# Attention and a two-layer feed-forward product: the second product of three token blocks as seven block products

## The chip, the cores and the metric

The kernel runs on one core of one Trainium2 chip. The metric is the time of one execution on the device in microseconds (us). Engines are called as the profile calls them: PE (matrix engine, PEld its weight loads), DVE (vector), ACT (scalar), POOL (GpSimd), SP (the queue that issues nearly all DMAs).

## The reference

Chunked attention gives x (3072 tokens by 512), and x goes through two matrix products with a piecewise activation in between. All is float32.

```python
out[:, :, c_start:c_end] = softmax(scale * q_c @ k_full^T) @ v_full   # 32 queries, 64 keys with 8 memory keys, head size 64
...
h = x @ w_in                                   # (3072, 512) @ (512, 2048)
g = np.where(h >= 1, h, np.where(h <= -1, 0.0, (h + 1) ** 2 / 4.0))
return g @ w_out                               # (3072, 2048) @ (2048, 512)
```

## The kernel before

**Tiles.** Tokens go in six blocks of 512. The 2048 middle columns are 16 chunks of 128, and four of them make a "quad" (q 0 to 3; m = 2q and 2q+1 are pairs of an even and an odd chunk). Each float32 operand is held as a high part and a rest, both in the matrix engine's reduced format, and each product is three: high by high, high by rest, rest by high. `weights` (L175) finds a chunk's weights, all of which lie in SBUF for the whole run in 16 tiles `wr` (printed as `wr_<number>`).

**Blocks 0 and 1** are worked with eight block products for everything, in the order of the table `FIRST` (L27). That stage also decodes the weights (`decode`, L184) and, in `build` (L563, letter t in the table), forms four combinations of each pair of w_in chunks and writes them to HBM as `saved`.

**Blocks 2 to 5** run the table `QUADS` (L61), one string per quad, through `quad` (L765). The first product (x by w_in) uses the seven-product scheme: `product` (L665) multiplies one sum of x's quarters (`A11`, `A12`, `A22`, `S1` to `S4`, made by `sum_up` and `split`, L642 and L647) with one w_in piece or combination. Such a product is 12 matmuls of 256 columns, seven to a quad. Three of the seven pieces are resident; the other four (products 6, 5, 7, 4) are loaded from `saved` by `load_t` (L591) into places of w_in that are no longer needed ("holes", L550), each load in two DMAs of 256 KB whose rows end as 1 KB pieces.

All seven go to two PSUM banks, X and Y (`PROD`, L51): `copy_out` (L711, ACT) copies X after products 1, 6 and 7, `add_up` (L719, DVE) adds Y, `relus` (L724) is three ACT operations, `join` (L735) one on DVE. The product that adds to a bank next waits for those that read it.

The second product (g by w_out) splits each g tile (128 by 512) into high part (`high`, L740, ACT) and rest (`low`, L746, DVE), and `pe_out` (L684) multiplies with eight products: 12 matmuls of 512 columns for one g tile, 16 tiles to a block. In the table it stands between the products of X and Y, and covers their waits; most of it belongs to the same quad or the one before. Results gather in four PSUM banks, and `store` and `last_store` (L519, L526) copy them out. The attention of the next block (`attention`, L405; its two PE parts are `pe_scores` and `pe_values`) is strewn between.

**What sets the order.** `InOrder` (L81) keeps every engine in the order in which the code emits, so the tables set the order on each engine; SP's DMAs too go one after the other, and one that waits holds those behind it. Since all operations go through it, the profile gives L89 for nearly all.

Of the kernel before, what the change touches and what calls it, by code (L numbers as in the profile page):

```python
# [16 lines left out]
P = 128  # L17
# [7 lines left out]
SECOND = 2  # L25

# [19 lines left out]
    F11 F12 n3 n3 F13 F13 F11 + n3 F12 n3 F13 n3 n3 n2 F14 F14 F14 n3 F13 F15 F12 n3 + F14 F13 F14  # L46
    n3 n2 F13 F15 F15 F15 F15 n3
# [13 lines left out]
QUADS = (  # L61
    """
    @S0 -h12 p1 p2 -g22 0 -l12 c1 p6 a11 0 -g12 p5 r11 0 z0 dS4 c2 m11 p7 kS4 c3 h11 a22 0 -g21 r22
    z1 m22 l11 h22 p4 r21 0 p3 a12 l22 0 0 r12 m21 h21 l21 g11 m12
    """,
    """
    p1 -h12 p2 0 0 c1 a11 0 -g21 p6 c2 -l12 0 r11 m11 0 -g22 p7 p5 0 @V0 c3 -g12 a22 h11 r22 p4 p3
    0 m22 h22 l11 a12 r12 g11 @S1 l22 r21 m21 h21 l21 m12
    """,
    """  # L70
    1 p2 p1 c1 1 a11 -g22 r11 m11 1 1 1 p6 p5 -h12 c2 -g21 p7 -l12 -g12 c3 h11 a22 1 r22 l11 m22 1
    h22 p4 l22 r21 p3 m21 h21 1 a12 r12 m12 1 g11 1 l21 1
    """,
    """
    p1 p2 c1 1 p6 -g22 -g21 c2 a11 1 kA11 @V1 r11 kA12 1 -h12 p7 m11 -l12 h11 c3 p5 dS3 a22 p4 p3
    dS1 r22 dS2 l11 m22 h22 -g12 g11 l22 a12 kA22 r21 m21 r12 m12 h21 kS3 kS2 l21 kS1
    """,
)
# [16 lines left out]
def attn_ffn_kernel(ctx: ExitStack, tc: tile.TileContext, first_qk, first_v, qk, vw, w, out):  # L95
# [34 lines left out]
    def two_banks(tag, name):  # L130
        return ps_2.tile([P, 2, 512], F32, name=name, tag=tag)
# [52 lines left out]
    def decode(i):  # L184
# [15 lines left out]
        hi, lo = ws[i][:, 0:n2], ws[i][:, n2 : 2 * n2]  # L200
# [204 lines left out]
    def attention(key):  # L405

        pe_scores(key)
        yield
# [5 lines left out]
        pe_values(key)  # L414
        yield
# [19 lines left out]

    items = []

    def half_step(blk, half, fc):
# [8 lines left out]
        for i, (m, x, cc) in enumerate(terms):  # L447
            pe.matmul(hp, m[:, cc * P : (cc + 1) * P], x[:, cc], start=i == 0, stop=i == len(terms) - 1)
# [24 lines left out]
        for t in range(2):  # L473
            ts, to = slice(t * P, (t + 1) * P), acc[blk][2 * half + t]
            for i, (a, m) in enumerate(((gh, wh), (gh, wl), (gl, wh))):
                pe.matmul(to, a[:, ts], m, start=fc == 0 and i == 0, stop=False)
        yield

    def step(blk, fc):
# [5 lines left out]
        for i, (m, x, cc) in enumerate(terms):  # L485
            pe.matmul(hp, m[:, cc * P : (cc + 1) * P], x[:, cc], start=i == 0, stop=i == len(terms) - 1)
# [39 lines left out]
    def last_store(t):  # L526

        src = acc[NB - 1][t]
        r0 = (NB - 1) * TB + t * P
        if t == 1:  # L530
            for i, (copy, queue) in enumerate(((dve.tensor_copy, sp), (act.copy, act))):
                cols = slice(i * DM // 2, (i + 1) * DM // 2)
                ob = apool.tile([P, DM // 2], F32, name="ob", tag=("pr", "f")[i], bufs=1 + i)
                copy(ob, src[:, cols])
                queue.dma_start(out[r0 : r0 + P, cols], ob)
        else:
            ob = apool.tile([P, DM], F32, name="ob", tag={2: "qk", 3: "v", 0: "pt"}[t])
            (act.copy if t == 3 else dve.tensor_copy)(ob, src)
            sp.dma_start(out[r0 : r0 + P, :], ob)

# [9 lines left out]
    hole_of = {}  # L550
    for i, n in ((0, 0), (1, 2), (2, 4), (3, 6)):
        for s in range(2):
            hole_of[i, s] = 2 * (n + s) + 1

    def hole(i, s):
        j, k = place[0, hole_of[i, s]]
        w = ws[j].rearrange("p (a b c) -> p a b c", a=2, b=2)
        return w[:, :, k, 0:HQ]

    saved = dram.tile([NFC // 2, P, 4, 2, HQ], F32, name="saved")  # L560
    ahead = {}

    def build(m):  # L563
# [5 lines left out]
        fef = apool.tile([P, 2, 2, HQ], F32, name="fef", tag="f", bufs=2)  # L569
        for j in range(2):  # L570
            hi, lo = (weights(0, 2 * m + j, part).bitcast(F32) for part in range(2))
            dve.tensor_tensor(fef[:, j].rearrange("p a b -> p (a b)"), hi, lo, op=ALU.add)
            yield
        b11, b21, b12, b22 = (fef[:, j, k] for j in range(2) for k in range(2))
        tf = apool.tile([P, 4, HQ], F32, name="tf", tag="f", bufs=2)
        dve.tensor_tensor(tf[:, 1], b12, b11, op=ALU.subtract)
        yield
        dve.tensor_tensor(tf[:, 2], b22, b12, op=ALU.subtract)
        yield
        dve.tensor_tensor(tf[:, 0], b22, tf[:, 1], op=ALU.subtract)  # L580
        yield
        dve.tensor_tensor(tf[:, 3], b21, tf[:, 0], op=ALU.subtract)
        yield
        st = ahead["y0"].tile([P, 4, 2, HQ], F32R, name="st", tag="st")
        act.copy(st[:, :, 0], tf)
        yield
        dve.tensor_tensor(st[:, :, 1], tf, st[:, :, 0].bitcast(F32), op=ALU.subtract)
        sp.dma_start(saved[m], st.bitcast(F32))
        yield

    def load_t(i, q):  # L591
        for s in range(2):
            sp.dma_start(hole(i, s).bitcast(F32), saved[2 * q + s, :, i])
# [3 lines left out]
    def side(name):  # L597
        if name not in part_of:
            if name in ("A11", "A12"):
                both = ahead["y0"].tile([P, 2, 2, 2, HQ], F32R, name="sa", tag="st")  # L600
                part_of["A11"], part_of["A12"] = both[:, 0], both[:, 1]
            else:
                pool = ahead["y0" if name == "S2" else "y1"]
                part_of[name] = pool.tile([P, 2, 2, HQ], F32R, name=name.lower())
        return part_of[name]

    def x_plain(key):

# [46 lines left out]
    def stationary(i, q, s, part):  # L655
        m = 2 * q + s
        if i == 1:
            return weights(0, 2 * m, part)[:, 0:HQ]
        if i == 2:
            return weights(0, 2 * m, part)[:, HQ : 2 * HQ]  # L660
        if i == 3:
            return weights(0, 2 * m + 1, part)[:, HQ : 2 * HQ]
        return hole(PROD[i][2], s)[:, part]

    def product(i, q):  # L665
        to, name, _ = PROD[i]
        x = side(name)
        for s in range(2):
            terms = [(0, 0, cc) if lo == 0 else (0, 1, cc) for cc in range(2) for lo in range(2)]
            terms += [(1, 0, cc) for cc in range(2)]  # L670
            for n, (wp, xp, cc) in enumerate(terms):
                pe.matmul(
                    bank[to][:, s * HQ : (s + 1) * HQ],
                    stationary(i, q, s, wp)[:, cc * P : (cc + 1) * P],
# [4 lines left out]
                )  # L679

# [286 lines left out]
```

## Time and profile before

| | us |
|---|---|
| median of 3 runs | 600.39 (599.39 to 600.58) |
| the profiled execution | 599.33 |
| its span, first to last instruction | 597.6 |

Busy over the span: PE 579.3, PEld 501.4, DVE 395.5, ACT 333.0, POOL 0.7 us. Block 2's first product starts at about 224 us; blocks 2, 3 and 4 then repeat every 93 us.

A row of the grouped instructions reads: line, engine, operation, output<-inputs, shapes, count | busy time, mean ns of one | idle time of the engine before it. A matmul's own duration holds the time of its results' way out; what a stream of matmuls costs is read from the chain of work, whose rows are start, length, engine and count. A row of the stretches gives, for each engine, busy us and the number of instructions, then the granted clock of PE, the busy share of the 16 DMA engines, and GB/s.

### The profile page before, as it was taken

The numbers are of one execution on the slowest core, as the hardware profiler recorded it, in microseconds if no ns is written. First come the engines' busy times: TensorE is split into PE (matmuls) and PEld (weight loads), VectorE is DVE, ScalarE is ACT, GpSimd is POOL, SyncE is SP. The second block draws the span as 40 slices with busy tenths as digits, with TensorE's granted clock in tenths as the row PEclk, the third lists the DMA queues.
The fourth block names the chain that finished last, engine by engine and source line by source line (L and its number), as shares of the span: only waits on it lengthen the run. The fifth ranks groups of instructions, "written<-read, shape, count | busy, mean of one in ns | idle before, by whom it ended". The sixth has DMA issues, their size and how long they took to land.

```text
span 597.6 us, 13941 instructions
## 1 busy us (share of the span) xinstructions
PE 579.3 (97%) x6072; PEld 501.4 (84%) x6072; DVE 395.5 (66%) x595; ACT 333.0 (56%) x587; POOL 0.7 (0%) x6
## 2 busy tenths in 40 slices
PE   5799999999999999999999999999999999999996
PEld 2788788888787889888898989988998988888984
DVE  5899999988889776735765735765735564523332
ACT  2589945456545466554574544665645556644651
POOL 0000000000000000000000000000000000000000
PEclk8589999999999999999999999999999999999999
DMA  8999102324345658366126465224552301533201
GB/s 353 422 421 420 41 15 92 135 69 189 141 177 210 250 148 306 113 191 200 35 73 203 124 203 178 70 73 142 176 175 70 111 2 35 177 114 95 76 0 70
DMA packets 39435, 91.06 MB, mean 152 GB/s; under 512 B 2896, under 2 KB 29776, under 8 KB 33744
## 3 DMA queue, kind: packets, MB, share of 16 engines
q1 hardware_dynamic: 39232, 90.06, 43.5%
q8 instruction: 47, 0.77, 0.5%
q10 hardware_dynamic: 144, 0.13, 0.1%
q14 instruction: 12, 0.10, 0.0%
HBM read 75.50 MB, written 14.68 MB: 151 GB/s over the span
## 4 chain that ended last, share of the span: by engine, by line
PE 83%; DVE 11%; ACT 3%; issue 2%; DMA 1%; DVEq 0%
PE ps_o L89 40%; PE ps_h L89 36%; DVE f L89 4%; PE ps_x L89 4%; PE ps_s L89 3%; DVE wr L89 2%; DVE gw L89 1%; DVE gl L89 1%; ACT w L89 1%; DVE pr L89 1%; DMA qk<-in_first_qk_dram 1%; DVE pt L89 1%; DVE ob L89 1%; DVE den L89 1%; ACT gw L89 0%
## 5 line engine op out<-in xcount | busy, mean ns | idle before, releaser
L89 PE MATMUL ps_o<-wr,gh 128*128 128x512 f32 x768 | 241.4, 395 | 1.6 <-DVE ob L89 1.6
L89 PEld LDWEIGHTS ps_o<-wr,gh 128*128 128x128 f32 x768 | 139.7, 188 | 30.8 <-DVE ob L89 2.4
L89 PE MATMUL ps_o<-wr,gl 128*128 128x512 f32 x384 | 151.6, 395 | 0.0
L89 PE MATMUL ps_h<-s,wr 128*128 128x256 f32 x768 | 100.2, 283 | 1.4 <-ACT u L89 1.4
L89 PEld LDWEIGHTS ps_h<-s,wr 128*128 128x128 f32 x768 | 96.5, 188 | 4.2 <-ACT u L89 2.0
L89 DVE SCALAR_TENSOR_TENSOR gw<-gw,gt 128x512 f32<-128x512 f32 (+1 forms) x88 | 56.0, 638 | 56.1 <-ACT gw L89 55.7
L89 PE MATMUL ps_h<-xth,wr 128*128 128x512 f32 (+1 forms) x320 | 91.4, 360 | 0.0
L89 PEld LDWEIGHTS ps_o<-wr,gl 128*128 128x128 f32 x384 | 72.2, 188 | 17.1 <-DVE gl L89 0.2
L89 DVE TENSOR_TENSOR gl<-gw,gh 128x512 fp32r<-128x512 f32 (+1 forms) x104 | 66.8, 643 | 23.4 <-ACT gh L89 23.1
L89 ACT CAST gh<-gw 128x512 fp32r<-128x512 f32 (+1 forms) x104 | 60.7, 589 | 35.1 <-DVE gw L89 34.9
L89 PEld LDWEIGHTS ps_h<-xth,wr 128*128 128x128 f32 x320 | 58.7, 197 | 9.8 <-ACT gt L89 0.5
L89 ACT ACTIVATE gw<-gw 128x512 f32<-128x512 f32 (+1 forms) x104 | 61.8, 594 | 0.0
L89 PE MATMUL ps_h<-xtl,wr 128*128 128x512 f32 (+1 forms) x160 | 55.9, 360 | 0.1
L89 PE MATMUL ps_h<-sa,wr 128*128 128x256 f32 x384 | 49.2, 283 | 0.0
L89 PEld LDWEIGHTS ps_h<-sa,wr 128*128 128x128 f32 x384 | 47.7, 188 | 1.4
L89 ACT ACTIVATE gw<-ps_h 128x512 f32<-128x512 f32 (+1 forms) x56 | 30.1, 537 | 28.3 <-PE ps_h L89 19.2
L89 DVE TENSOR_TENSOR gt<-gt,ps_h 128x512 f32<-128x512 f32 x32 | 22.0, 686 | 34.0 <-ACT gt L89 20.8
L89 ACT COPY gt<-ps_h 128x512 f32<-128x512 f32 x32 | 18.8, 587 | 42.4 <-PE ps_h L89 42.2
L89 DVE STREAM_TRANSPOSE pt<-pr 32x512 f32<-32x512 f32 (+1 forms) x60 | 41.5, 700 | 1.3
L89 DVE SCALAR_TENSOR_TENSOR f<-w,f 128x1024 uint32<-128x1024 uint32 x32 | 38.7, 1219 | 0.1
L89 ACT ACTIVATE gw<-gt 128x512 f32<-128x512 f32 x32 | 20.2, 633 | 28.9 <-DVE gt L89 28.9
L89 PEld LDWEIGHTS ps_h<-xtl,wr 128*128 128x128 f32 x160 | 31.7, 198 | 4.7 <-DVE xtl L89 0.3
(63 smaller groups left out, 524.3 us busy)
## 6 DMA issues: line engine op xcount, KB each, us to landing
wr<-saved SPq DMA_DIRECT2D x104, 256.0 KB, 3.9
w<-in_w_dram SPq DMA_DIRECT2D x16, 1024.0 KB, 19.9
qk<-in_qk_dram SPq DMA_DIRECT2D x10, 1536.0 KB, 6.9
v<-in_vw_dram SPq DMA_DIRECT2D x10, 1024.0 KB, 5.8
saved<-st SPq DMA_DIRECT2D x8, 1024.0 KB, 4.0
out_dram<-ob SPq DMA_DIRECT2D x23, 256.0 KB, 3.3
qk<-in_first_qk_dram SPq DMA_DIRECT2D x4, 768.0 KB, 8.7
v<-in_first_v_dram SPq DMA_DIRECT2D x4, 512.0 KB, 12.4
```

The lines of the kernel that those rows point to most:

```text
L89: return self.tc.keep_in_program_order(getattr(self.engine, name)(*args, **kwargs))
```

## The change

- **Second product of blocks 3, 4 and 5.** It becomes the seven-product scheme too, by units of half a block (256 tokens) and a quad: eight units a block. In a unit (`unit`), POOL forms four sums of g's quarters (`gs`), ACT and DVE split four operands into high part and rest (`gsa`, `gsb`, `gsc`, `gsd`), and PE does seven products of 6 matmuls of 256 columns, into seven half banks. After four units, `drain` adds the seven sums up with one ACT copy and seven DVE additions of 128x256, and stores. Block 2 keeps eight products.
- **Half a block behind.** A block's units run under the first product of the rest of that block and of the next. The first half's g tiles stay in SBUF (`gk`); the second half's go to HBM (`plain_g`) and come back (`gr`).
- **Combinations of w_out** (`build_out`, tokens T0 to T7): on POOL, six operations per pair, then three ACT and three DVE operations. They take places of w_in and w_out, so from block 3 on all seven w_in pieces of a product are streamed through a ring of four places, each load one DMA of 512 KB in rows of 4 KB. Block 2 still streams four of seven, in two DMAs of 256 KB. `build` now writes all seven pieces to `saved`.
- **Order.** `QUADS` gives way to one list, `PLAN`, of 1,160 steps for blocks 2 to 5. In block 3 quads 1 and 2 are interleaved, quad 1 with two PSUM banks of its own (`ps_g`). `FIRST` loses one load; the v tiles of later blocks share a place with qk and are loaded after `pe_scores`.
- The values of w tiles lie as alternating runs of 256 (high, rest), so a 512-column matmul of blocks 0 to 2 reads its moving operand in two runs (`wide`).

```diff
-QUADS = (
-    """
-    @S0 -h12 p1 p2 -g22 0 -l12 c1 p6 a11 0 -g12 p5 r11 0 z0 dS4 c2 m11 p7 kS4 c3 h11 a22 0 -g21 r22
...
+PLAN = """
...
+    30a11 30p5 T4 T4 30c2 30p7 3kS4 23l22 T4 T4 T4 4x 4x 30r11 4x 3jS4 4x 4x T4 T4 T4 30c3 30a22 T5
...
+    30r12 30m12 3u0s3 32p1 31p1 31c1 32c1 31p2 4x 3u0s1 3u0s2 31p6 31c2 4x 31a11 31r11 31m11 31p5
...
+    def build_out(m):
+        e, o = 2 * m, 2 * m + 1
+        fef = apool.tile([P, 2, 2, HQ], F32, name="feo", tag="f", bufs=2)
+        for j in range(2):
+            hi, lo = (weights(1, e + j, part).bitcast(F32) for part in range(2))
+            pool.tensor_tensor(fef[:, j], hi, lo, op=ALU.add)
+            yield
+        b11, b12, b21, b22 = (fef[:, j, k] for j in range(2) for k in range(2))
+        for to, x, y in ((b11, b12, b11), (b12, b22, b12), (b22, b22, b11), (b21, b21, b22)):
+            pool.tensor_tensor(to, x, y, op=ALU.subtract)
+            yield
...
+        for src, hi, lo in homes:
+            act.copy(hi, src)
+            yield
+            dve.tensor_tensor(lo, src, hi.bitcast(F32), op=ALU.subtract)
+            yield
+    NRING = 4
+    def load_ahead():
+        while len(loaded) < len(stream) and free(len(loaded)):
...
+                sp.dma_start(to.bitcast(F32), saved[q, :, KEPT[i]].rearrange("p s a c -> p (s a c)"))
-    def load_t(i, q):
-        for s in range(2):
-            sp.dma_start(hole(i, s).bitcast(F32), saved[2 * q + s, :, i])
...
     def product(blk, i, q):
...
+        if streamed(blk, i):
+            passed.append((q, i))
+        done.add((blk, i, q))
+        load_ahead()
...
+    def unit(u, op):
...
+            a, b, how, to = {
+                "3": (lambda: ge[:, :, 0], lambda: ge[:, :, 1], ALU.subtract, 0),
+                "1": (lambda: ge[:, :, 1], lambda: go[:, :, 1], ALU.add, 1),
+                "2": (lambda: S[:, 1], lambda: ge[:, :, 0], ALU.subtract, 2),
+                "4": (lambda: go[:, :, 0], lambda: S[:, 2], ALU.subtract, 3),
+            }[op[1]]
+            pool.tensor_tensor(S[:, to], a(), b(), op=how)
...
+                act.copy(it[k][0], src)
...
+                dve.tensor_tensor(lo, src, hi.bitcast(F32), op=ALU.subtract)
...
+        for s in range(2):
...
+            w = taken(2 * q + s, i)
+            for n, (g, part) in enumerate(((hi, 0), (hi, 1), (lo, 0))):
...
+                pe.matmul(dst, g, w[:, part], start=first, stop=True, skip_group_check=True)
+    def drain(blk, half, op):
...
+        if op == "0":
+            act.copy(c21, p[1])
+            return
...
+        dve.tensor_tensor(dst, a, p[i], op=ALU.add)
```

How the rows of the engines' programs move is shown at three places. On PE before, in the first quad of block 5: the last two products of X and Y (`a` is A22, `s` is S4) and the second product around them, with g's parts `gh` and `gl`.

```order
L89 MATMUL ps_o<-wr_1440,gh 128x512 x2
L89 MATMUL ps_o<-wr_1440,gl 128x512
L89 MATMUL ps_h<-a_2635,wr_1109 128x256 x6
L89 MATMUL ps_h<-a_2635,wr_1392 128x256 x6
L89 MATMUL ps_h<-s_2802,wr_1109 128x256 x6
L89 MATMUL ps_h<-s_2802,wr_1392 128x256 x6
L89 MATMUL ps_o<-wr_1143,gh 128x512 x2
L89 MATMUL ps_o<-wr_1143,gl 128x512
```

On PE in the changed program, at the end of the same quad (`s` is S4 of block 5, `a` its A11 for the next quad); the rows with `gsc` and `gsd` belong to units of block 4's second half.

```order
L140 MATMUL ps_h<-s_2874,wr_1116 128x256 x12
L140 MATMUL ps_o<-wr_547,gsd 128x256 x3
L140 MATMUL ps_o<-wr_632,gsd 128x256 x3
L140 MATMUL ps_o<-wr_632,gsc 128x256 x3
L140 MATMUL ps_o<-wr_770,gsc 128x256 x3
L140 MATMUL ps_h<-a_2524,wr_1399 128x256 x12
L140 MATMUL ps_o<-wr_770,gsd 128x256 x3
L140 MATMUL ps_o<-wr_832,gsd 128x256 x3
L140 MATMUL ps_o<-wr_792,gsd 128x256 x3
L140 MATMUL ps_o<-wr_895,gsd 128x256 x3
```

The second product now comes in threes of 256 columns, and between two products of X and Y stand one or more units' products of six matmuls.

On SP in the changed program, within block 4's last quad: `wr` rows are the ring's loads, `gr` is the second half's g coming back, and the store is of block 3's second half. Before, this stretch held `wr` loads of 256 KB and the loads of qk and v.

```order
L140 DMA wr_1399<-saved 128x1024
L140 DMA wr_895<-saved 128x1024
L140 DMA gr<-plain_g 128x1024
L140 DMA out_dram<-ob 128x2x512
L140 DMA wr_972<-saved 128x1024
L140 DMA wr_1116<-saved 128x1024
```

The g tiles (their way out, `plain_g`, a few rows earlier) and stores stand among the ring's loads in one queue, each with a wait of its own.

On POOL in the changed program, where the building of w_out's combinations (`feo`) meets the first units' sums (`gs`); before, POOL has nothing after the first 2 us.

```order
L140 TENSOR_TENSOR feo<-feo 128x256 x4
L140 TENSOR_TENSOR gs<-gk 128x256 x2
L140 TENSOR_TENSOR gs<-gs,gk 128x256
L140 TENSOR_TENSOR gs<-gk,gs 128x256
L140 TENSOR_TENSOR feo<-wr_1150 128x512
L140 TENSOR_TENSOR feo<-wr_1399 128x512
L140 TENSOR_TENSOR feo<-feo 128x256 x2
```

Six of the eight buildings stand before the first sums, the last two among them.

More of the change, by code (lines that the diff above doesn't have):

```diff
@@ L81 @@
+"""
 class InOrder:
@@ L750, in begin_second, with parts_of @@
+    def parts_of(token):
+        head, op = re.match(r"(\d+|[TL]\d)(.*)", token).groups()
+        return head, op
+    plan = [parts_of(token) for token in PLAN.split()]
+    for head, op in plan:
+        if op[:1] == "p" and streamed(int(head[0]), int(op[1])):
+            stream.append((order[int(head[0])][int(head[1])], int(op[1])))
     def begin_second():
-        for i in (0, 1, 2, 3):
-            load_t(i, 0)
+        load_ahead()
         let_go("x1")
+        let_go("early_v")
         ahead["y1"] = hold("y1", "left")
@@ L814, in left @@
[L814 to L834 removed]
+    chains = {}
@@ new lines, in advance, with left, planned @@
+    def advance(name, start):
+        if name not in chains:
+            chains[name] = start()
+        next(chains[name], None)
+    def left(which):
+        if which == 2:
+            for _ in chains[f"F{NFC - 1}"]:
+                pass
+            return
+        for _ in range(2):
+            next(chains[f"F{NFC - 2 + which}"], None)
+    def planned(head, op):
+        if head[0] == "L":
+            left(int(head[1]))
+            return
+        if head[0] == "T":
+            advance(head, lambda: build_out(int(head[1])))
+            return
+        blk = int(head[0])
+        if len(head) == 1:
+            what, which = op[0], op[1:]
+            if what in "xy":
+                advance(head + what, lambda: attention((blk, "xy".index(what))))
+            elif what in "DE":
+                drain(blk, "DE".index(what), which)
+            elif what == "z":
+                store(blk, int(which))
+            elif what == "d":
+                sum_up(which)
+            elif what in "kj":
+                split(which, "h" if what == "k" else "l")
+            elif what == "u":
+                n = int(which[0])
+                unit((blk, n // NQ, order[blk][n % NQ]), which[1:])
+            return
+        q, what, which = order[blk][int(head[1])], op[0], op[1:]
+        key = (blk, q)
+        if what == "p":
+            product(blk, int(which), q)
+        elif what == "c":
+            copy_out(int(which), key)
+        elif what == "g":
+            pe_out(*key, which)
+        else:
+            {"a": add_up, "r": relus, "m": join, "h": high, "l": low}[what](which, key)
@@ L873, in attn_ffn_kernel @@
     begin_second()
-    for blk in range(SECOND, NB):
-        for n in range(NQ):
-            quad(blk, n)
-    finish()
+    for head, op in plan:
+        planned(head, op)
+    close_ps("singles")
+    let_go("y0")
+    let_go("y1")
 def weight_order(n):
```

453 lines of the change are left out of this document (292 added, 161 removed).

## The prediction

> **What bounds the kernel now.** I read the page's busy times first, then the shares of the chain, then the stretches of 93 us in which blocks 2 to 5 repeat, with PE's waits in them.
>
> ```profile
> PE 579.3 (97%) x6072; PEld 501.4 (84%) x6072; DVE 395.5 (66%) x595; ACT 333.0 (56%) x587; POOL 0.7 (0%) x6
> PE 83%; DVE 11%; ACT 3%; issue 2%; DMA 1%; DVEq 0%
> 226.00:319.00 93.00, 93.00 (x1048) 83.27 (x1047) 56.84 (x85) 53.28 (x94) 0.00 (x0) 1.00 0.48 156
> 319.00:412.00 93.00, 92.55 (x1042) 82.58 (x1041) 55.17 (x82) 51.91 (x93) 0.00 (x0) 1.00 0.44 137
> 412.00:505.00 93.00, 92.55 (x926) 82.97 (x925) 52.81 (x80) 51.58 (x91) 0.00 (x0) 1.00 0.32 92
> 505.00:597.60 92.60, 86.69 (x517) 75.97 (x515) 32.48 (x50) 43.49 (x77) 0.00 (x0) 1.00 0.30 91
> PE ps_h L89 <- ACT u L89: 1.4, 3, 0.5
> PE ps_o L89 <- DVE ob L89: 0.8, 1, 0.8
> ```
>
> The reader sees one engine full: in blocks 2 to 4 PE is busy 92.6 to 93.0 of 93 us at clock 1.00, DVE 57 to 61%, ACT 55 to 57%, and in all of 226 to 590 us PE waits 2.2 us. So here a matmul less is time less, as long as the others keep up. A busy PE says little about its rate, so that comes from the chain of work.
>
> ```profile
> 492.33 5.58 PE ps_o L89 x24
> 572.00 5.70 PE ps_h L89 x48
> 222.26 1.48 PE L89 MATMUL ps_s<-qk 64*32 64x64 f32 x128
> 254.93 2.07 PE L89 MATMUL ps_x<-pt,v 64*64 64x32 f32 x128
> ```
>
> A 512-column matmul costs 5.58/24 = 0.2325 us, a 256-column one 5.70/48 = 0.1188, 2% over half. Half a block's attention has one of each of the last two rows, 3.55. A block is then 336 x 0.1188 + 192 x 0.2325 + 2 x 3.55 = 39.9 + 44.6 + 7.1 = 91.7 of its 93.
>
> **PE's saving.** In blocks 3 to 5, 576 matmuls of 512 columns become 1,008 of 256: 133.9 us become 119.8, so 14.2 us go, and blocks 3 and 4 need 86.9 us. The first product, block 2's second one and the attention keep their counts. Could a group of six matmuls cost more than a share of a long stream? These rows say no:
>
> ```profile
> 236.51 1.59 PE L89 MATMUL ps_h<-a,wr 128*128 128x256 f32 x12
> 237.93 1.58 PE L89 MATMUL ps_h<-s,wr 128*128 128x256 f32 x12
> ```
>
> The groups start 1.42 apart, 0.1183 a matmul; 1.59 holds the last result's way out. The 576 matmuls of 512 columns that stay in blocks 0 to 2 read their operand in two runs: I cost that at nothing; at most it is what two matmuls of 256 cost over one of 512, 0.005, or 2.9 us in all.
>
> **The end.** Twice at the end PE waits for a copy, since two sums share a tile's banks:
>
> ```profile
> 586.83 0.72 PE L89 MATMUL ps_o<-wr,gh 128*128 128x512 f32 x2 [0.78 <-DVE ob L89]
> 592.08 0.73 PE L89 MATMUL ps_o<-wr,gh 128*128 128x512 f32 x2 [0.78 <-DVE ob L89]
> 593.34 0.39 PE L89 MATMUL ps_o<-wr,gl 128*128 128x512 f32 x1
> 594.62 0.38 ACTq L89 DMA_DIRECT2D out_dram<-ob  x1
> out_dram<-ob SPq DMA_DIRECT2D x23, 256.0 KB, 3.3
> ```
>
> The change drains by half banks while other products run, so 1.6 us go. What is late next: after the last product, one DVE addition (about 0.4) and two stores of 256 KB, the second 0.36 behind the first. From PE's end at 593.73 that is 0.05 + 0.4 + 0.1 + 0.36 + 3.3 = 4.2 us, where the span ended 3.9 after it: 0.3 back.
>
> **What ACT, DVE and POOL get.**
>
> ```profile
> L89 DVE TENSOR_TENSOR gl<-gw,gh 128x512 fp32r<-128x512 f32 x88 | 60.2, 684 | 22.7 <-ACT gh L89 22.4
> L89 DVE TENSOR_TENSOR gl<-gw,gh 128x256 fp32r<-128x256 f32 x16 | 6.6, 417 | 0.6 <-ACT gh L89 0.6
> L89 ACT CAST gh<-gw 128x512 fp32r<-128x512 f32 x88 | 54.2, 620 | 30.2 <-DVE gw L89 30.1
> L89 ACT CAST gh<-gw 128x256 fp32r<-128x256 f32 x16 | 6.6, 416 | 4.9 <-DVE gw L89 4.8
> L89 DVE COPY ob<-ps_o 128x512 f32<-128x512 f32 x12 | 8.2, 688 | 24.4 <-PE ps_o L89 22.9 <-DMA out_dram<-ob 1.5
> masks.py:199 POOL TENSOR_SCALAR_AFFINE_SELECT ident<-ident 128x128 f32<-128x128 f32 x1 | 0.3, 295 | 0.1
> ```
>
> - A unit splits three operands of 512 and one of 256 where half a block's quad had two of 512: DVE +0.684 + 0.417 = 1.10, ACT +0.620 + 0.416 = 1.04; a block (eight units) +8.8 and +8.3. Draining adds 14 x 0.417 - 2 x 0.688 = 4.5 a block on DVE. Block 4, from the row 319 to 412: DVE 55.2 + 13.3 = 68.5 of 86.9 (79%), ACT about 60 (69%). Both stay off the path in the mean: cost nothing, but their waits have less cover.
> - Building w_out's combinations: 0.684 + 2 x 0.417 = 1.5 on DVE and as much on ACT for each of eight, in blocks 2 and 3.
> - POOL's additions are not in the trace. Below: DVE's 0.417 and 0.684; above: POOL's one operation of this family, 0.295 per 128 columns, so 0.59 and 1.18. With 128 additions of 256 and 16 of 512 that is 64 to 94 us; I take the upper end, the same engine's row: 18.9 in a block's 86.9, plus 4.7 per building. Its work alone bounds nothing.
>
> The Trainium skill ("GPSIMD Engine Reference", section "Elementwise — side-by-side cycle accounting") gives 4497 against DVE's 2293 ns for an addition of 2048 values; by that ratio these would be 0.82 and 1.34, an estimate of 126 us in all, still a quarter of the engine's time in a block.
>
> **The weights' stream.**
>
> ```profile
> 25.00:45.00 20.00, 17.97 (x226) 16.56 (x226) 18.87 (x30) 16.40 (x32) 0.00 (x0) 0.87 1.01 422
> 510.00:520.00 10.00, 10.00 (x63) 8.94 (x62) 5.16 (x8) 7.41 (x14) 0.00 (x0) 1.00 0.83 257
> wr<-saved SPq DMA_DIRECT2D x104, 256.0 KB, 3.9
> qk<-in_qk_dram SPq DMA_DIRECT2D x10, 1536.0 KB, 6.9
> SPq L89 <- PE ps_h L89: 195.0, 88, 33.5
> L89 SPq DMA_DIRECT2D wr<-saved x104: 359/360/2043, 215.6 to 557.9; - x104
> ```
>
> A full DMA share carries 422/1.01 = 418 GB/s in the rows of 8 KB that the first stage loads, and 257/0.83 = 310 in the present 1 KB pieces. A block of 3 or 4 moves 28 loads of 0.524 MB, 5.2 of qk and v, 4.2 of g out and back, 1.05 of results: 25.2 MB, 60 us at one rate and 81 at the other, of 86.9. For rows of 4 KB I take 380: 66 us, so the stream is hidden in the mean. One load lands in 3.9 - 0.85 + 1.25 = 4.3 us at the better rate, 4.7 at the lower. A place frees four products ahead, so a load has at least three products, 4.3 us; that minimum occurs where eight products of quads 1 and 2 of block 3 stand in a row, and costs 0 to 2 us. Elsewhere a product comes every 86.9/28 = 3.1 us, with 9 us of cover. SP issues 64 more DMAs at 0.36, but it idles 195 us for PE alone. The v tiles now wait for `pe_scores`, and the next qk for `pe_values`: counted in `PLAN` at these rates, 8.5 to 15.7 us of PE work lie between `pe_values` and the next `pe_scores`, over qk's 6.9 to landing. A load of 1.5 MB, a store or a g tile that waits in SP's order holds the ring's next loads behind it; if that cover fails, it is the second rival.
>
> The first stage writes 14.7 MB for 8.4 to HBM; 6.3/0.31 = 20 us more of DMA in a stretch with shares of 0.46 and 0.63 (rows below): hidden, at worst 2 us late for block 2's qk.
>
> ```profile
> 150.00:200.00 50.00, 50.00 (x577) 40.29 (x577) 43.07 (x73) 26.73 (x44) 0.00 (x0) 1.00 0.46 174
> 200.00:250.00 50.00, 50.00 (x515) 43.23 (x514) 37.68 (x57) 27.02 (x48) 0.00 (x0) 1.00 0.63 218
> 571.83 3.00 PE L89 MATMUL ps_h<-s,wr 128*128 128x256 f32 x24
> 573.46 0.59 ACT L89 COPY gt<-ps_h 128x512 f32<-128x512 f32 x1 [3.31 <-PE ps_h L89]
> ```
>
> **New waits on PE.** A product on X waits for the copy of X: the last two rows show it start 0.2 us after the product's 12 matmuls (571.83 + 1.43) and take 0.59, so with the way back about 1.0 us. One other product (1.42) covers that if ACT is free; behind a `relus` triple (1.9) it lacks up to 1.0 + 1.9 - 1.42 = 1.5. Counting in both orders the products with under 2.2 us of other PE work since the last on their bank, I find 12 before and 20 now, with ACT and DVE fuller. If none of the 20 waits: 0; if all lack the whole: 30. Before, such places cost next to nothing, so I take a quarter: 7.5 us. Behind a waiting product stand the units' products, and behind those ACT's and DVE's next work.
>
> **The sum**, on the profiled execution: 599.3 - 14.2 - 1.6 + 0.3 = 583.8, plus 7.5 = 591.3. That execution lies 1.06 under the median of three, at the low end of their spread; I add 0.2: **591.5**.
>
> **Rivals.**
> 1. *The order holds* (0.19). Waits stay under 4 us, as PE's 2.2 us over four blocks now would have it: 584 to 588. Against it: the shorter blocks with more of ACT and DVE.
> 2. *Weights come late* (0.13). Eleven loads of qk and v go in front of the ring. At 310 GB/s DMAs are at 81 of 86.9 us and a third of these meet a short lead, 3 us each: 11, and 2 for the row of eight: 583.8 + 13 and half the bank waits: 595 to 601.
> 3. *POOL stops DVE* (0.14), the slower side. Nearly all splits and joins on DVE read two SBUF operands, as POOL's additions do. If each POOL operation held DVE for its whole length, block 3 would be 55.2 + 13.3 + 3.0 of DVE and 18.9 + 2 x 4.7 of POOL, 99.8 against 86.9: 12.9 over; block 2 56.8 + 6 x 1.5 + 6 x 4.7 = 94.0 against 91.7: 2.3 over; block 4 52.8 + 13.3 + 18.9 = 85.0: nothing. 583.8 + 15.2 and half the bank waits: 603. It decides once POOL costs DVE over (86.9 - 71.5)/28.3 = 54% of its own time in block 3. For it, nothing in the trace, where POOL never runs beside DVE; against it, that POOL can run while DVE is idle or reads PSUM. The Trainium skill ("SBUF — State Buffer", section "Who interferes with whom") states the rule: a DVE instruction with two SBUF inputs and a POOL instruction that reads SBUF exclude each other, and the later one waits for the whole of the earlier. No run here shows it; by that rule both would wait in turn, which is why this rival has more than a token chance.
> 4. *A 256-column matmul in small groups costs more* (0.04): at 0.133 (1.59/12) the 1,008 cost 134 and nothing is saved: 605. The two rows of 1.42 above speak against it.
>
> **How the numbers follow.** My forecast (waits of 4 to 12 us, 588 to 596) has 0.50. A measurement of this kernel tells about 0.2% (1.2 us) from no change. Faster than 599.2: 0.50 + 0.19 + 0.10 of rival 2 = 0.79; within 0.2%: 0.05, from the upper part of rival 2 and the lowest of rival 3; slower: 0.16. The range from 584 to 603 takes in both ends of the bank waits up to 19 us and leaves out half of rivals 3 and 4 and a little below.
>
> **What would show it.** Right: units of 42 matmuls in 5.0 us on the chain; blocks 3 and 4 each about 87 to 90 us; PE's waits in them short and for ACT or DVE at `ps_h`; `wr<-saved` of 512 KB landing in under 5 us; DVE's `gsc` and `gsd` splits at 0.68. Rival 2: PE or its loads waiting for `wr<-saved`. Rival 3: splits well over 0.684 beside POOL, DVE near 95%. Wrong altogether: 256-column streams slower than 0.12 us, or a first stage that ends later than 224 us.

## The result, and the profile after

The changed kernel takes **603.12 us** (median of 7 runs, 601.34 to 605.67) where the kernel before took 599.62 beside it: ratio 1.006, 95% interval 1.004 to 1.0081. It is slower by 0.6%; the forecast was 591.5, faster. The profiled execution took 604.34, its span 602.6.

The page's busy times of the changed kernel and the shares of its chain:

```profile
PE 572.8 (95%) x6504; PEld 518.2 (86%) x6504; DVE 474.6 (79%) x710; ACT 360.8 (60%) x667; POOL 142.0 (24%) x150
PE 76%; DVE 14%; ACT 4%; issue 3%; DMA 1%; DVEq 0%; ACTq 0%
```

Three stretches of it (window, length, busy us and instructions of PE, PEld, DVE, ACT, POOL, then granted clock, DMA share, GB/s):

```profile
223.00:303.00 80.00, 76.55 (x957) 69.02 (x956) 60.37 (x81) 47.74 (x88) 27.17 (x24) 1.00 0.50 167
303.00:390.00 87.00, 83.53 (x1059) 77.84 (x1058) 65.58 (x97) 55.68 (x106) 37.68 (x37) 1.00 0.75 259
390.00:480.00 90.00, 84.67 (x1145) 82.59 (x1144) 73.50 (x108) 56.50 (x106) 29.41 (x32) 0.99 0.84 276
```

PE, full before, now stands still for 3.5 us of the first stretch, 3.5 of the second and 5.3 of the third. No other engine is full: DVE is 75 to 82% busy in each.

DVE's groups between 225 and 600 us:

```profile
L140 DVE SCALAR_TENSOR_TENSOR gw<-gw,gt 128x512 f32<-128x512 f32 x36 | 30.2, 840 | 13.3 <-ACT gw L140 13.2
L140 DVE TENSOR_TENSOR gt<-gt,ps_h 128x512 f32<-128x512 f32 x30 | 20.5, 682 | 21.7 <-ACT gt L140 12.8 <-PE ps_h L140 7.1 <-ACT gk L140 1.6
L140 DVE TENSOR_TENSOR gsc<-gs,gsc 128x512 fp32r<-128x512 f32 x24 | 19.9, 832 | 4.2 <-ACT gsc L140 4.2
L140 DVE TENSOR_TENSOR gsa<-gk,gsa 128x256 fp32r<-128x256 f32 x12 | 7.8, 668 | 0.9 <-ACT gsa L140 0.9
L140 DVE TENSOR_TENSOR ob<-ob,ps_o 128x256 f32<-128x256 f32 x42 | 16.9, 417 | 5.0 <-ACT ob L140 3.5 <-PE ps_o L140 0.5
```

Two of POOL's, from the page:

```profile
L140 POOL TENSOR_TENSOR feo<-wr 128x512 f32<-128x512 f32 x16 | 23.2, 1470 | 290.3 <-DMA out_dram<-ob 241.7
L140 POOL TENSOR_TENSOR gs<-gk 128x256 f32<-128x256 f32 x24 | 22.3, 942 | 97.2 <-DMA out_dram<-ob 29.2
```

Instructions whose two operands lie in SBUF have become longer (`gw` 840 and `gsc` 832 ns for the 684 of 128x512, `gsa` 668 for 417); those with one in PSUM have not (`gt` 682, `ob` 417). POOL's too take longer than the 0.59 and 1.18 us of the forecast.

PE's waits in blocks 2 to 5 (total, times, longest), the largest three and the one for weights:

```profile
PE ps_o L140 <- issue: 3.3, 1, 3.3
PE ps_h L140 <- DVE gt L140: 2.7, 2, 2.1
PE ps_x L140 <- issue: 1.9, 1, 1.9
PE ps_g L140 <- DMA wr<-saved: 0.5, 1, 0.5
```

The chain at the first of them:

```profile
475.27 0.67 PE ps_o L140 x4
475.94 3.32 issue
479.26 0.80 PE ps_o L140 x2
480.06 2.56 PE ps_h L140 x12
```

Weights come late once, by 0.5 us. The longest wait is for nothing that the profile shows ("issue"): it falls in the middle of a group of six matmuls whose operands are there, the first four of the six being done. Right behind it PE is also slow: the last row's 12 matmuls are 2.56/12 = 0.213 us apart, not 0.1186, and the granted clock from 480 to 485 us is 0.51. That costs about 2.6 us more; the row of the stretch, in the layout above, shows it as a clock of 0.98:

```profile
480.00:590.00 110.00, 108.47 (x883) 107.36 (x882) 74.03 (x113) 67.36 (x127) 44.42 (x50) 0.98 0.61 197
```

How far did PE's own part come as forecast? A unit's stream on the chain reads

```profile
550.46 4.98 PE ps_o L140 x42
```

and 4.98/42 = 0.1186, as reckoned. From the starts of all matmuls after 223 us, with 0.2326 and 0.1186 for the two lengths: the streams are 343.6 us before and 329.2 after, 14.4 less. Attention's small matmuls, with the waits among them, take 19.8 and 24.1, and the rest, PE waiting or running at the lower clock, 7.2 and **21.6**. The saving is real; 14.4 and 4.3 us more come back in these two.

### The profile page after: what moved, and what is told of

Same layout as the page of the kernel before. It is cut to its first block, busy times and chain, and to the rows that moved or that the text cites. A ratio compares the mean times of both kernels' runs of the same rounds, so it can differ in the third digit from the quotient of the medians.

```text
span 602.6 us, 15457 instructions
## 1 busy us (share of the span) xinstructions
PE 572.8 (95%) x6504; PEld 518.2 (86%) x6504; DVE 474.6 (79%) x710; ACT 360.8 (60%) x667; POOL 142.0 (24%) x150
## 4 chain that ended last, share of the span: by engine, by line
PE 76%; DVE 14%; ACT 4%; issue 3%; DMA 1%; DVEq 0%; ACTq 0%
PE ps_h L140 36%; PE ps_o L140 34%; PE ps_x L140 3%; PE ps_s L140 2%; ACT gw L140 2%; DVE gw L140 1%; DVE pr L140 1%; DVE gl L140 1%; DVE den L140 1%; PE ps_g L140 1%; DVE f L140 1%; DVE ob L140 1%; DVE gt L140 1%; DVE pt L140 1%; DMA wr<-saved 1%
## 5 line engine op out<-in xcount | busy, mean ns | idle before, releaser
L140 PE MATMUL ps_o<-wr,gh 128*128 128x512 f32 x384 | 120.8, 396 | 0.0
L140 PE MATMUL ps_h<-s,wr 128*128 128x256 f32 x720 | 95.5, 285 | 3.0 <-DVE gt L140 2.7
L140 PEld LDWEIGHTS ps_h<-s,wr 128*128 128x128 f32 x720 | 90.4, 191 | 4.8 <-DVE gt L140 3.6
L140 POOL TENSOR_TENSOR feo<-wr 128x512 f32<-128x512 f32 x16 | 23.2, 1470 | 290.3 <-DMA out_dram<-ob 241.7
L140 PE MATMUL ps_h<-xth,wr 128*128 128x512 f32 (+1 forms) x320 | 91.6, 361 | 0.0
L140 PEld LDWEIGHTS ps_o<-wr,gh 128*128 128x128 f32 x384 | 70.5, 188 | 14.9
L140 PE MATMUL ps_o<-wr,gl 128*128 128x512 f32 x192 | 75.9, 396 | 0.6 <-DVE gl L140 0.6
L140 PE MATMUL ps_h<-a,wr 128*128 128x256 f32 x540 | 71.2, 284 | 1.5 <-ACT gk L140 0.8
L140 PEld LDWEIGHTS ps_h<-a,wr 128*128 128x128 f32 x540 | 68.2, 190 | 2.8 <-ACT gk L140 1.0
L140 PEld LDWEIGHTS ps_h<-xth,wr 128*128 128x128 f32 x320 | 58.8, 197 | 9.8 <-ACT gt L140 0.5
L140 DVE SCALAR_TENSOR_TENSOR gw<-gw,gt 128x512 f32<-128x512 f32 (+1 forms) x76 | 53.0, 700 | 17.9 <-ACT gw L140 17.7
L140 PE MATMUL ps_h<-xtl,wr 128*128 128x512 f32 (+1 forms) x160 | 56.0, 361 | 0.1
L140 ACT ACTIVATE gw<-ps_h 128x512 f32<-128x512 f32 (+1 forms) x55 | 29.6, 539 | 39.6 <-PE ps_h L140 30.8
L140 ACT CAST gh<-gw 128x512 fp32r<-128x512 f32 (+1 forms) x56 | 31.3, 563 | 35.5 <-DVE gw L140 32.4
L140 ACT ACTIVATE gw<-gw 128x512 f32<-128x512 f32 (+1 forms) x80 | 47.1, 589 | 0.0
L140 POOL TENSOR_TENSOR gs<-gk 128x256 f32<-128x256 f32 x24 | 22.3, 942 | 97.2 <-DMA out_dram<-ob 29.2
L140 PEld LDWEIGHTS ps_o<-wr,gl 128*128 128x128 f32 x192 | 36.1, 188 | 9.8 <-DVE gl L140 1.3
L140 DVE STREAM_TRANSPOSE pt<-pr 32x512 f32<-32x512 f32 (+1 forms) x60 | 41.4, 699 | 1.4
L140 DVE TENSOR_TENSOR gl<-gw,gh 128x512 fp32r<-128x512 f32 (+1 forms) x56 | 37.2, 667 | 5.9 <-ACT gh L140 5.5
L140 PE MATMUL ps_o<-wr,gsc 128*128 128x256 f32 x288 | 40.3, 285 | 0.6 <-DVE ob L140 0.3
L140 PE MATMUL ps_o<-wr,gsd 128*128 128x256 f32 x288 | 39.8, 282 | 0.2 <-DVE gsd L140 0.2
L140 DVE SCALAR_TENSOR_TENSOR f<-w,f 128x1024 uint32<-128x1024 uint32 x32 | 38.7, 1216 | 0.1
## 6 DMA issues: line engine op xcount, KB each, us to landing
w<-in_w_dram SPq DMA_DIRECT2D x16, 1024.0 KB, 19.8
```

What stands on the lines that cost most here:

```text
L140: return self.tc.keep_in_program_order(getattr(self.engine, name)(*args, **kwargs))
```

## The experiments

Three theories. **T1**: POOL's additions hold up DVE's instructions with two SBUF operands, and PE waits for what DVE does later. **T2**: denser DMA traffic delays something that PE needs, the supply of instructions above all. **T3**: the new order's short covers alone, with ACT and DVE fuller. Times are medians beside the kernel before on the same chip (its medians 599.4 to 599.9); ratios are to it, with 95% intervals.

**1. No additions on POOL.** The splits of `gsc`, `gsd` and of w_out's combinations read a resident weight tile.

```diff
-            pool.tensor_tensor(S[:, to], a(), b(), op=how)
-            pool.tensor_tensor(fef[:, j], hi, lo, op=ALU.add)
-            pool.tensor_tensor(to, x, y, op=ALU.subtract)
```

> Leaves out all of POOL's additions (the combinations of g and those of w_out); the splits that read them read a resident weight tile instead, so the output is not the reference's, and DVE, ACT, PE and the DMAs do the same operations at the same places of the order. T1 (POOL beside DVE lengthens DVE's instructions with two SBUF operands, and PE's waits grow from that): gl, gw, gsc, gsd back to 684 ns, gsa to 417, DVE busy 475 -> about 447 us; the waits at 247, 291, 343 us go, time 590 to 594, at most 597 if the long wait near 476 us and the half clock behind it stay. T2 (instructions reach PE late because data DMAs are dense: 3.5 us at 476, 2 at 353, and 2.8 of half clock): DVE faster, time still 599 to 603. T3 (the new order's short covers alone, with ACT and DVE fuller): PE's waits stay near 20 us, 601 to 603.

593.56 us, ratio 0.9882 (0.9847 to 0.9916). The profiled execution is the quickest of six, 587.0; the other five took 592.9 to 595.9 and left no profile. Its busy times and one of its groups:

```profile
PE 564.6 (96%) x6504; PEld 512.9 (88%) x6504; DVE 440.6 (75%) x710; ACT 360.5 (62%) x667; POOL 0.7 (0%) x6
```

```profile
L140 DVE TENSOR_TENSOR gsc<-wr,gsc 128x512 fp32r<-128x512 f32 x24 | 16.4, 685 | 6.3 <-ACT gsc L140 6.3
```

The splits of 128x512 are back at 685, DVE is 34 us less busy, and 9.5 us are gone. That speaks for T1, and against T3 as the main cause.

**2. POOL adds, nobody reads.** The same kernel with POOL's additions put back.

> POOL does all its additions as in the changed kernel, but nothing reads their results (the splits read the same resident weight tile as in the kernel without additions, so the output is not the reference's): the only difference to that kernel is that POOL is busy 142 us. T1 by the interference alone: DVE busy 470 or more, time as the changed kernel's, 601 to 604. T1 by the other half (what is late is POOL's results, since an addition takes 0.8 to 1.5 us where I had reckoned 0.59 and 1.18): time as without additions, 590 to 597. T2 and T3: no difference to the kernel without additions, both 599 to 603.

605.93 us, ratio 1.0114 (1.0089 to 1.014); DVE 475.8. Between this kernel and the last only POOL differs, and nothing waits for POOL's results: 12.4 us are interference.

**3. POOL writes but hardly reads.**

```diff
-            pool.tensor_tensor(S[:, to], a(), b(), op=how)
+            pool.tensor_copy(S[:, to, 0, 0:1], a()[:, 0, 0:1])
+            for _ in range(2):
+                pool.memset(S[:, to], 0.37)
```

> From the kernel whose sums are unread (605.9; without POOL 593.6): each addition on POOL becomes a copy of one column, which keeps its start tied to the same data, and two fills of the same tile, so POOL is busy and writes SBUF but hardly reads it; the output is not the reference's. If it is POOL's reading that lengthens DVE's instructions, splits back near 0.69 us and 593 to 596; if a busy POOL of any kind does it, splits stay at 0.75 to 0.86 and 602 to 606.

594.94 us, ratio 0.9909 (0.9877 to 0.9941). Busy times and the same group:

```profile
PE 566.9 (96%) x6504; PEld 515.3 (87%) x6504; DVE 440.7 (74%) x710; ACT 360.6 (61%) x667; POOL 125.6 (21%) x406
```

```profile
L140 DVE TENSOR_TENSOR gsc<-wr,gsc 128x512 fp32r<-128x512 f32 x24 | 16.4, 685 | 6.4 <-ACT gsc L140 6.4
```

POOL is busy 126 us and DVE notices nothing: it is POOL's reading. The fills are also shorter than the additions (0.31 and 0.53 us), but that alone doesn't explain it: in experiment 9 additions of about 0.41 us still cost DVE 21 us.

**4. The additions on DVE**: all of them, those of `build_out` alone, those of the units alone.

```diff
-            pool.tensor_tensor(S[:, to], a(), b(), op=how)
+            dve.tensor_tensor(S[:, to], a(), b(), op=how)
```

> The same sums, issued on DVE at the same places of the order; nothing left out. DVE gets 96 + 32 additions of 128x256 at 0.417 and 16 of 128x512 at 0.684, 64 us, and loses the interference: 447 + 64 = 511 us, 85% of the span. T1: what POOL takes from DVE (27 us) and its own slowness are worth more than the queueing, 594 to 599. T3 (a fuller DVE is what makes PE wait): slower than the changed kernel, 605 to 612. T2: 601 to 604.

> The additions that build w_out's combinations (16 of 128x512, 32 of 128x256, in blocks 2 and 3) go to DVE at their places in the order, those of the units stay on POOL; nothing left out. DVE +24 us in blocks 2 and 3, less the interference there. T1 by the interference: the waits at 247, 291 and 343 us (4.2 us) go, 597 to 602. T1 turned round (a DVE that queues, as with all sums on DVE, 611): 604 to 609. T2: no change, 602 to 604.

> The other half: the units' 96 additions of 128x256 go to DVE at their places, w_out's combinations stay on POOL; nothing left out. All on DVE was 8.2 us slower than the changed kernel. If the queueing on DVE is what that cost, most of it lies here, where DVE is 74 of 90 us in block 4: 605 to 610. If POOL's interference in block 4 and 5 is what the change suffers from, 598 to 602.

611.3 (1.0199, 1.0181 to 1.0217), 604.68 (1.0074, 1.0051 to 1.0097) and 608.88 us (1.0152, 1.0117 to 1.0186). My expectation for the first was a miss. With all on DVE no instruction is lengthened, yet DVE is busy 494.9 and the sums stand in its queue ahead of what PE waits for (`PE ps_o L140 <- DVE ob L140: 2.9, 4, 2.0`). That fits a DVE whose total matters less than what stands ahead of the operation that PE needs; a run that moves the sums to other places on DVE was not made.

**5. Half of the streamed bytes.**

```diff
-                sp.dma_start(to.bitcast(F32), saved[q, :, KEPT[i]].rearrange("p s a c -> p (s a c)"))
+                sp.dma_start(to[:, 0 : n2 // 2].bitcast(F32), saved[q, :, KEPT[i]].rearrange("p s a c -> p (s a c)")[:, 0 : n2 // 2])
```

> Each of the 84 streamed loads of 512 KB brings only the first half of its rows (2 KB of 4 KB, 256 KB a load), the rest of the place keeps old weights, so the output is not the reference's: DMA share in blocks 3 and 4 from 0.75 to 0.84 down to about 0.5, same number of DMAs. T2 (instruction supply behind dense data): the waits marked issue on PE (5.9 us) and the half clock (2.8) go, 594 to 597. Late weights: 601 to 602.5, since PE's waits on wr<-saved sum to 0.5 us. T1 and T3: 602 to 604.

596.7 us, ratio 0.996 (0.9945 to 0.9974). PE's waits marked issue (this view of this kernel):

```profile
PE ps_s L140 <- issue: 1.6, 1, 1.6
PE ps_o L140 <- issue: 1.3, 1, 1.3
```

2.9 us where the changed kernel has 7.5, with DVE as slow as there (474.3). The row on `ps_s` lies in the first stage, as 1.1 us of the kernel before do; behind 223 us the changed kernel has 5.9 and this one 1.3. The slow matmuls are gone too, the granted clock is 1.00:

```profile
480.00:590.00 110.00, 107.50 (x893) 106.39 (x893) 75.85 (x116) 65.16 (x123) 44.48 (x50) 1.00 0.41 130
```

So traffic is a second cause, worth 6.4.

**6. Neither POOL's additions nor the other half of the bytes**: edits 1 and 5 together.

> The kernel without POOL's additions and with half of every streamed load of 512 KB: both parts that moved the time, 603.1 to 593.6 (POOL away) and 603.1 to 596.7 (half the bytes), taken out together; the output is not the reference's. If the two are separate, their gains add: 9.5 + 6.4 = 15.9, time 587, and what stays over the 583.8 that PE's work alone gives is the new order's own waits, about 3 us. If they are one (DVE late and instructions late hide each other, or dense DMA is what slows DVE), 590 to 593.

584.7 us, ratio 0.9741 (0.971 to 0.9773). The gains add, with 2.5 us to spare (15.9 expected, 18.4 found), and what stays is 0.9 above the 583.8 that PE's work alone gave in the forecast: with both causes out, the new order's own waits, T3, are about 1 us.

**7. The rows.** Two loads of 256 KB in rows of 2 KB; then one load of 512 KB in rows of 2 KB and of 1 KB, by another layout of `saved` (the one for 1 KB also shortens the rows that `build` writes and block 2 loads).

```diff
-                sp.dma_start(to.bitcast(F32), saved[q, :, KEPT[i]].rearrange("p s a c -> p (s a c)"))
+                for s in range(2):
+                    cols = slice(s * (n2 // 2), (s + 1) * (n2 // 2))
+                    sp.dma_start(to[:, cols].bitcast(F32), saved[q, :, KEPT[i]].rearrange("p s a c -> p (s a c)")[:, cols])
```

> Each streamed load of 512 KB in rows of 4 KB becomes two loads of 256 KB in rows of 2 KB, same bytes to the same places, nothing left out: undoes one part of the change. If the long rows make instructions and other transfers wait, 599 to 602. If it is the amount of data that does it, 603 to 606: shorter rows take longer, and SP issues 84 DMAs more. If rows matter to nothing, 602 to 604.

> Rows of 2 KB with still one load of 512 KB for each product: only the layout of the saved weights in DRAM changes. With two loads of 256 KB in such rows 599.5, with one in rows of 4 KB 603.1. If the length of a row decides, 598 to 600.5; if what helped was that a load is cut in two, 602 to 604. PE's waits marked issue (7.5 us in the changed kernel, 3.4 with two loads) go the same way.

> The same with rows of 1 KB, as the kernel before streams them: one load of 512 KB a product. If short rows let instructions through, 597 to 600 unless the loads then land too late: at the 310 GB/s that rows of 1 KB gave before, a load takes about 5.5 us to land and DMAs are near 0.95 busy in block 4, PE waits for wr<-saved by several us and the time is 602 to 608.

599.46 (0.9991, 0.9968 to 1.0013), 599.88 (1.0015, 0.9986 to 1.0044) and 601.98 us (1.0027, 1.0002 to 1.0052). Rows of 2 KB give back 3.2 to 3.7 us whether a load is cut or not, though the single load's runs spread from 598.2 to 606.1; the gain of about 1 us from rows of 1 KB isn't clear of noise. PE's issue waits in these profiles are 3.4, 4.9 and 4.9 us.

**8. POOL beside the kernel before.** Four additions of 128x112 after each `low`, reading `gl`.

```diff
+        for n in range(4):
+            cols = gl[:, n * 112 : (n + 1) * 112].bitcast(F32)
+            pool.tensor_tensor(gpool.tile([P, 112], F32, name="extra", tag="extra", bufs=1), cols, cols, op=ALU.add)
```

> The kernel before, with 256 additions of 128x112 on POOL that read each gl tile of blocks 2 to 5 after its split and write a scratch tile nobody reads; the output stays the reference's. POOL busy some 130 us where DVE is 57 to 61% busy. If POOL's reading costs DVE its own length as in the changed kernel, gl and gw lengthen by 0.05 to 0.15 us each, DVE 396 -> 415 to 430; time 600 to 603, since DVE has slack there. If the interference needs the changed kernel's fuller DVE, no longer instructions, 599 to 600.

598.39 us, ratio 0.9979 (0.9958 to 1.0): no cost. The groups of POOL and of `gl`:

```profile
L89 POOL TENSOR_TENSOR extra<-gl 128x112 f32<-128x112 f32 x256 | 115.7, 452 | 469.6 <-DVE den L89 263.3 <-DVE gl L89 190.7
L89 DVE TENSOR_TENSOR gl<-gw,gh 128x512 fp32r<-128x512 f32 x64 | 45.3, 708 | 21.0 <-ACT gh L89 17.1 <-POOL extra L89 3.8
```

POOL reads for 116 us and DVE's `gl` grows by 23 ns, DVE in all by 4 us, where the changed kernel's 142 us cost it 34. So POOL's busy time is not what counts. Its single instruction is shorter here (452 ns), but so are those of 0.41 us in experiment 9, which cost DVE 21 us; that it starts when DVE has just finished a `gl` is the reading left, which no run tests alone.

**9. Shorter instructions on POOL.** Pieces of 128x128 for 128x256 and 128x512, nothing else; then with rows of 2 KB as in 7; then pieces of 128x64 with those rows.

```diff
-            pool.tensor_tensor(S[:, to], a(), b(), op=how)
+            a, b = a(), b()
+            for n in range(2):
+                pool.tensor_tensor(S[:, to, n], a[:, n], b[:, n], op=how)
```

> Every addition on POOL becomes additions of 128x128 (two for 128x256, four for 128x512), same results, nothing left out. Undisturbed, POOL took 0.735 us for 128x256 and 0.37 for 128x112, so POOL gets about a quarter more work. If a DVE instruction waits for the rest of the one POOL instruction that runs (and POOL's next one then waits for it), the wait of each of the 75 that were held is about halved: DVE 475 -> 457 to 462 us, time 596 to 600. If the two share the operands' port by busy time, POOL's longer work costs more: DVE 480 or more, 603 to 606.

> The same halves on POOL and, besides, streamed weights in rows of 2 KB as two loads of 256 KB; nothing left out. If both gains are what they seem and add, 3.7 below the kernel with halves alone: 593 to 597, under both the kernel before and the changed one. If halves don't help, 599 to 603.

> Rows of 2 KB and POOL's additions in pieces of 128x64, some 0.3 us each, so POOL is busy near 200 us; nothing left out. If only the length of one instruction counts, DVE 450 to 456 us and 1 to 3 us under the kernel with halves and rows of 2 KB, 591 to 595. If the many starts make up for it, or the units wait for POOL's sums, that kernel's time or up to 5 us more.

595.87 (0.9933, 0.9918 to 0.9947), **592.6** (0.9885, 0.9868 to 0.9903) and 609.17 us (1.015, 1.0132 to 1.0168). Busy times and a group with pieces of 128x128, rows of 4 KB:

```profile
PE 568.9 (96%) x6504; PEld 516.0 (87%) x6504; DVE 460.7 (78%) x710; ACT 360.8 (61%) x667; POOL 184.7 (31%) x326
```

```profile
L140 POOL TENSOR_TENSOR feo<-feo 128x128 f32<-128x128 f32 x64 | 36.0, 596 | 0.0
```

POOL is busier by 43 us and DVE less by 14: the length of one POOL instruction matters more than POOL's busy time. In the trace, 74 DVE instructions of the changed kernel started while a POOL addition ran and took at least 0.05 us longer than without POOL, 0.53 us in the mean; with pieces of 128x128 it is 93 of 0.34, with 128x64 110 of 0.28. A hold gets shorter, but there are more of them: below 128x128 DVE gains nothing (461.7 us busy), where I had expected 450 to 456. The smallest pieces lose time for another reason: POOL is busy 242 us, and its results come late (waits of ACT, pieces of 128x64):

```profile
ACT gsc L140 <- POOL gs L140: 16.5, 8, 4.7
ACT gsd L140 <- POOL gs L140: 15.7, 10, 4.4
```

In the changed kernel the first of these rows is 4.4. The kernel with pieces of 128x128 and rows of 2 KB, which leaves nothing out, is the fastest of those that give the reference's output, 1.15% under the kernel before.

**10. The changed kernel again.**

> The changed kernel once more, unaltered, beside the kernels with the two edits and under a second profile. If it is what it was: 602 to 604, DVE 474 to 476 us, PE's waits marked issue 5 to 8 us with the longest at the same matmul (number 5553 of 6504). If the first profile's issue waits were chance, 2 to 4 us.

602.59 us, ratio 1.0046 (1.0028 to 1.0064), DVE 473.0, issue waits 5.6 us, the longest (2.4) at the same matmul as in the first profile.

## Why the prediction was wrong

**Right: PE's saving and, within 0.3 us, the end.** The sum without waits was 583.8; with neither cause the kernel takes 584.7. The streams shrink by 14.4 us for 14.2, and from PE's end to the span's are 4.5 us for 4.2. Matmuls of 256 columns in small groups cost 0.1186 (rival 4 falls), the two-run operand nothing to be seen, the first stage ends at 223.0 us. Weights cost PE 0.5 us (and a load of qk 0.9 in the second profile), so rival 2, as it was put (PE waiting for `wr<-saved`), falls too.

**The failed step: "Its work alone bounds nothing".** From there POOL was costed at nothing, and rival 3, which has the true hold (POOL stops DVE) and nearly the true time (603), got 0.14. What was wrong is the test by which I weighed it: that POOL must fill DVE (54% of its own time in block 3) before it costs. Measured, 139 us of POOL cost DVE 35 (experiments 1 and 2), 25%, DVE was nowhere full, and 9.5 to 12.4 us were lost (12.0 with half the bytes). Even POOL's own time was put too low: an addition of 128x256 or 128x512 took 0.94 and 1.47 us, for 0.59 and 1.18 in the forecast. (By the 0.82 us of the prediction's second estimate, 32 additions are 30% of a block, not a quarter.) Not capacity but delay at single places costs time. The timeline of the changed kernel (start, us, engine, what, and in brackets the idle time before) shows how, in its rows of POOL and DVE from 243 us on and PE's last:

```profile
242.99 2.54 POOL L140 TENSOR_TENSOR feo<-wr 128x512 f32<-128x512 f32 x2 [241.69 <-DMA out_dram<-ob]
243.13 1.19 DVE L140 TENSOR_SCALAR den<-den 128x16 f32<-128x16 f32 x1
244.35 0.25 DVE L140 RECIPROCAL rin<-den 128x16 f32<-128x16 f32 x1
244.64 1.97 DVE L140 TENSOR_TENSOR pr<-pr,rin 128x1024 f32<-128x1024 f32 x1
245.49 1.73 POOL L140 TENSOR_TENSOR feo<-feo 128x256 f32<-128x256 f32 x1
246.65 0.71 DVE L140 STREAM_TRANSPOSE pt<-pr 128x512 f32<-128x512 f32 x1
247.18 2.95 POOL L140 TENSOR_TENSOR feo<-wr 128x512 f32<-128x512 f32 x2
247.28 1.70 DVE L140 SCALAR_TENSOR_TENSOR gw<-gw,u 128x512 f32<-128x512 f32 x1
248.91 0.68 DVE L140 TENSOR_TENSOR gt<-gt,ps_h 128x512 f32<-128x512 f32 x1
...
249.64 0.63 PE L140 MATMUL ps_h<-s,wr 128*128 128x256 f32 x3 [2.10 <-DVE gt L140]
```

`den` has 16 columns and takes 0.17 us in the kernel without POOL; here it takes 1.19, to the end of POOL's first instruction (242.99 + half of 2.54). `pr` (1.23 there) takes 1.97 and makes POOL's 128x256 wait in turn (1.73; POOL's quickest took 0.72), and POOL's next addition makes `gw` take 1.70 for 0.65. One after the other they put `gt` 2.8 us late (1.02 + 0.74 + 1.05), and the product on X has its cover used up. Without POOL's additions the same place reads

```profile
243.72 0.65 DVE L140 SCALAR_TENSOR_TENSOR gw<-gw,u 128x512 f32<-128x512 f32 x1
244.29 0.68 DVE L140 TENSOR_TENSOR gt<-gt,ps_h 128x512 f32<-128x512 f32 x1
245.61 2.65 PE L140 MATMUL ps_h<-s,wr 128*128 128x256 f32 x21
```

and PE goes on without a stop. The rule of the Trainium skill that the prediction weighed ("SBUF — State Buffer", section "Who interferes with whom") says just this: whichever of the two starts first keeps the shared ports for its whole instruction and the other fully blocks, a GpSimd instruction that only writes is free of it, and so is a DVE instruction with one operand in SBUF unless it runs in a mode that uses both ports. The traces agree: the timeline shows the first, 685 ns beside POOL's fills the second, 682 for `gt` with one operand in PSUM the third. That `den`, with one operand, was held fits if it ran in such a mode, which no row shows. I had the rule and asked of the engine's total what had to be asked of each wait.

**"The stream is hidden in the mean": true of the weights, not of the rest.** Traffic costs 6.4 us with POOL and 8.9 without (experiments 1, 5 and 6), though PE waits 0.5 for weights. What shows of it is, first, PE's issue waits: 7.5 and 5.6 us in two profiles for 2.9 and 2.1 with half the bytes. The longest lies between the same two matmuls (5553 and the next, counted from 0) in all 16 profiles of this PE program: 1.5 and 1.0 us in the two kernels with half the bytes, 1.7 to 3.7 in the other fourteen. The trace lists 51 transfers of 16 KB in a queue of their own:

```profile
q8 instruction: 51, 0.84, 0.6%
```

In the changed kernel one of them begins at 476.96 us and takes 0.93, while PE stands from 475.94 to 479.26, though it ends 1.4 us before PE goes on. Another, the thirtieth, begins at matmul 3774 or 3775 with half the bytes and at 3784 to 3909 in the other fourteen. That PE's instructions come late behind data is thus the reading that fits; it was only shown that fewer bytes shorten the waits. Why it is always this matmul stays open.

Second, the stops are followed by slow matmuls. Between 100 us and PE's last matmul the traces hold 21 stretches of 3.4 to 6.8 us at a granted clock of 0.5; 20 of them begin during a stop of PE of 1.7 us or more, or within 1.8 us behind it, while 12 other such stops have none behind them. The kernel before, the two kernels with half the bytes and the quickest execution of experiment 1 have no such stretch; what makes a stop lead to one, no run tests. Between the profiles of the changed kernel and of that with half the bytes (604.3 and 596.7) the issue waits differ by 4.6 us and the slow matmuls by about 2.6, nearly all of the 7.6. The 8.9 without POOL can't be traced so: the only profile of experiment 1 is its quickest execution, 1.4 us above that of experiment 6.

**Rows of 4 KB**, which I took as a help (380 GB/s), are part of it: 3.2 to 3.7 us worse than rows of 2 KB, and 3.3 in the pair of experiment 9. The Trainium skill ("Perfetto Trace Analysis", section "DMA Optimizations") recommends batching small transfers, as from 2 KB to 4 or 8 KB, where a kernel is bound by DMA; here PE bounds it, and the longer rows cost time. In the profiles of that pair the issue waits, 5.2 us against 6.2, and one stretch at half clock against two (some 1.5 us) hold most of the difference; by which way rows of 4 KB bring them about stays open.

**"New waits on PE", 7.5 us.** The term has the right place and a wrong source: 0.9 come from the order that it was meant for, some 10 to 12 from POOL's holds and 6 to 9 from traffic. A quarter of 30 could not be read off a trace in which neither was present. Taken as differences of the measured kernels, the parts are 583.8 + 0.9 + 12.0 + 6.4 = 603.1, a sum that holds by how they are taken. That rival 3's 603 meets the result is luck: it has 15.2 us for POOL from a DVE over-full in blocks 2 and 3, which was 75% busy there, and nothing for traffic.

## What to carry to other kernels

Work moved to POOL is not free because POOL and DVE are both half idle: where both read SBUF, each can hold the other for the rest of an instruction, so ask which DVE instructions stand just ahead of what the bounding engine waits for, and cut POOL's instructions to about the length of one that this chain can lose (here 128x128: 7 us gained; 128x64 was too small, as POOL's results came late). When a shorter instruction stream saves time on a full engine, count what else now flows per us: the data beside it and, if the reading of the issue waits holds, the engine's own instructions. And a rival whose mechanism is stated and whose price alone is open deserves an experiment or a wide range, not a token chance.

## What the runs showed of the hardware that I had not expected

- A DVE instruction on 16 columns (`den`) took 1.19 us beside POOL for 0.17 without: the hold goes by the length of POOL's instruction, not by DVE's own size.
- POOL's quickest additions in the traces take 0.72 us for 128x256, 1.26 for 128x512 and 0.37 for 128x112.
- POOL's fills (0.53 us for 128x512) and DVE's two-operand instructions don't disturb each other: DVE is busy 440.7 us beside them and 440.6 without POOL.
- PE can stand up to 3.7 us in the middle of a group whose operands are there, at the same matmul in all 16 profiles of this PE program.
- A stop of PE of 1.7 to 3.6 us was in 20 of 32 cases followed by 3.4 us or more at half the granted clock; in the changed kernel's first profile 3.3 us of standing were followed by about 2.6 more.
